# Another order of the first two batches, and q and k transposed in four transfers in place of six

## The chip, the cores and the metric

The kernel runs on one core of one Trainium2 chip. The metric is the device time of one execution in microseconds (us); lower is better. Of four runs of the kernel before, the median is 314.41 us (313.33 to 316.91).

The engines are called as in the profile: PE is TensorE (matmuls), PEld its loading of weights, ACT is ScalarE, DVE is VectorE, POOL is GpSimd, and SP is SyncE, which here only issues transfers. Each engine carries out its own instructions in order.

## The reference

Two layers follow each other. The first is attention over a sliding window, with a bias that falls with the distance; the second multiplies the result x by w_in, applies h * cos(h), and multiplies by w_out.

```python
B, H, S, D = 8, 8, 576, 64                       # q, k, v, float32
scores = scale * q @ k.T + bias                  # bias = -slope[h] * |i - j|
mask = (rel >= 0) & (rel < 128)                  # rel = i - j
attn = softmax(where(mask, scores, -1e9))
x = (attn @ v).transpose(0, 2, 1, 3).reshape(4608, 512)
h = x @ w_in                                     # 512 x 2048
out = (h * cos(h)) @ w_out                       # 2048 x 512
```

## The kernel before, in words

**Tiles.** A batch has 576 tokens: four blocks of 128 and a last one of 64. The 4608 tokens of all batches together are also cut into nine chunks of 512 for the second layer, so chunk c holds the end of one batch and the start of the next, and each chunk shifts by 64 tokens against the batches. Weights and inputs are cast to bf16 while they are loaded.

**Attention.** `load_nat` (line 450) brings q and k with tokens on the partitions, one block at a time, from POOL's queue. They are wanted with the head's 64 columns on the partitions. For batches 0 and 1 TensorE transposes them (`first_transposes`, line 532, and `first_tail`, line 558). For batches 2 to 7 `cross_transposes` (line 580) issues DMA transposes from SP: for each of q and k one transfer for blocks 0 and 1, one for blocks 2 and 3, and one for the short block 4 with its 64 rows. A batch's work is nine units (`units`, line 598): four pairs of heads for the first 256 tokens (G = 0), four for the next 256 (G = 1), and one tail. `scores` (line 608) multiplies for a whole group of units in one piece of PE work (the matmuls are on lines 629 and 619); `exps` (650) is on ACT, `mask` (671) on DVE, `pv` (696) on PE, `norm` (738) on DVE, and `x_back` (775) brings x back with its columns on the partitions: by PE in the first batches, and by a DMA transpose from SP (line 786, the tail line 778) from the second half of batch 2 on. Batches 2 to 7 run in three groups of three units. The second group holds the last pair of heads of G = 0 and the first two of G = 1; for G = 1 the scores need blocks 1 to 3 of k and 2 and 3 of q.

**Second layer.** `moe1` (line 830) multiplies a chunk by 128 columns of w_in in four matmuls of 512 tokens (line 835). `moe1_half` (line 842) does two times 128 columns for 256 of the chunk's tokens instead, in eight matmuls (line 850), so a chunk's first half can start before x of the second half is there. How many column pairs are done in halves is the tuple in the loop at the end (line 925). `gcu` (819) is cos on ACT and the product on DVE; `moe2_mm` (858) is the multiplication by w_out (line 861), and `store` (869) the way out.

**The order of the work.** `Plan` (line 109) sets it before the kernel runs. Each piece of work is written down by `op` with its engine, its reads and writes, a cost in ns (`occ`, `lat`) and a priority (`pri`, small first). `schedule` (198) places the pieces one by one at the earliest time at which an engine can take them, by those costs, and the order found is the fixed order of each engine's instructions. So where a transfer lands later than the plan had it, the engine stands still, and all that was placed behind it waits too. `Wires` (line 51) models the transfers: every packet of a transposing transfer costs 0.92 ns, or 1.45 where POOL's queue runs as well, whose packets cost 0.825 and more; SP is held while over 2000 of its packets are outstanding (RING). `pad` (170) fills PE's waits in the first 16 us with matmuls of zeros.

**Queues.** All loads but two come from POOL in the order of the list `FIRST`, then batch by batch (`load_batch`, line 900): batch 3 behind the last transpose of batch 2, later ones behind the x transposes of an earlier batch. SP issues the transposes of q and k, those of x, and the stores, in the order of the plan.

**The first two batches** follow three lists written out by hand: `HEAD` for batch 0 ("T" a transposition on PE, "R" a group of units with its PSUM slots, "E" the masks of the tail), `JOBS` for the sixteen `moe1_half` of chunk 0 (half, column pair, PSUM bank), and `SECOND` for batch 1 ("F" is the transposition of the short block).

Of the kernel before, what the change touches and what calls it, by code (L numbers as in the profile page):

```python
# [20 lines left out]
SPLIT = 4  # L21
VW = 66

ORDER, WAR, DATA = 0, 1, 2
FIRST = [("k", "q", 0, 1), ("h", "k"), ("h", "q"), ("v", 0, 0), ("v", 0, 1), ("k", "k", 0, 1),
         ("v", 0, 2), ("v", 0, 3), ("i", 6, 2), ("i", 2, 2), ("i", 4, 2), ("i", 0, 2),
         ("i", 12, 2), ("i", 8, 4), ("m",), ("i", 14, 2), ("k", "q", 1, 0), ("v", 0, 4),
         ("t", "k", 0), ("o", 0, 4), ("k", "k", 1, 0), ("t", "q", 0), ("o", 4, 4), ("o", 8, 4),
         ("v", 1, 0), ("v", 1, 1), ("o", 12, 2), ("o", 14, 2), ("v", 1, 2), ("k", "k", 1, 1),
         ("k", "q", 1, 1), ("t", "k", 1), ("t", "q", 1), ("v", 1, 4), ("v", 1, 3)]  # L30
HEAD = [("T", "k", 0, 0, 3), ("T", "q", 0, 2, 3), ("R", (3,), (1,)), ("T", "q", 1, 7, 6),
        ("R", (1,), (2,)), ("R", (0,), (0,)), ("R", (2,), (3,)), ("T", "k", 1, 1, 7),
        ("R", (4,), (0,)), ("E",), ("R", (7,), (3,)), ("R", (5,), (2,)), ("R", (6,), (1,))]
JOBS = [(0, 6, 6), (0, 1, 1), (0, 2, 3), (1, 4, 1), (0, 4, 2), (0, 3, 5), (1, 3, 3), (1, 2, 6),
        (0, 0, 4), (1, 1, 7), (1, 0, 0), (1, 7, 5), (1, 6, 2), (0, 7, 7), (0, 5, 3), (1, 5, 4)]
SECOND = [("T", "k", 0, 2, 2), ("F", 0, 6), ("T", "q", 0, 3, 3), ("R", (2,), (3,)),
          ("R", (9,), (1,)), ("R", (1,), (2,)), ("R", (3,), (3,)), ("T", "k", 1, 6, 6),
          ("T", "q", 1, 4, 4), ("R", (4,), (3,)), ("R", (0,), (1,)), ("R", (7,), (3,)),
          ("F", 1, 5), ("R", (5,), (2,)), ("R", (8,), (1,)), ("R", (6,), (2,))]
ENG = ("pe", "act", "dve", "pool", "sp")  # L40


# [8 lines left out]
class Wires:  # L51
# [4 lines left out]
    CROSS, MIXED = 0.92, 1.45  # L56
    RING = 2000
    LOADED = 3200

    def __init__(self):  # L60
        self.t = 0.0
# [30 lines left out]
    def add(self, o, e, st):  # L92
        if st > self.t:
            self.t, self.q, _ = self._step(self.t, self.q, st)
        n, cost, cross = o.pk
        late = self.LOADED if e != "pool" and self.q.get("pool") else 0
        self.q.setdefault(e, []).append([o, st + o.occ + self.DELAY[e] + late, n, cross, cost])
        _, _, done = self._step(self.t, self._copy(), 1e9)
        free = st + o.occ
        held = sum(x[2] for x in self.q[e])  # L100
        for d, de, t in done:
            d.end = t + (self.DONE if de != "pool" else min(2400, max(0, 0.17 * (t - 3000))))
            if de == e and e != "pool" and held > self.RING:
                held -= next(x[2] for x in self.q[e] if x[0] is d)
                free = max(free, t)
        return free


class Plan:
# [5 lines left out]
    COLD = 7000  # L115
    HEAD = 16000
    SLACK = 25
# [8 lines left out]
    def op(self, eng, fn, r=(), w=(), dma=None, occ=100, lat=None, pri=5, mode=0, table=None,  # L126
           pk=None, after=(), behind=()):
        o = Op()
        o.seq = len(self.all)
        o.eng = (eng,) if isinstance(eng, str) else tuple(eng)  # L130
        o.fn, o.r, o.w, o.dma = fn, tuple(r), tuple(w), dma
        o.occ, o.lat, o.pri, o.mode, o.table = occ, occ if lat is None else lat, pri, mode, table
        o.pk, o.banks = pk, {k[1]: None for k in o.w if k[0] == "B"}
        preds = {d: ORDER for d in behind}
        preds.update((d, DATA) for d in after)
        for k in o.r:
            if k in self.writer:
                preds[self.writer[k]] = DATA
        for k in o.w:
            if k in self.writer:  # L140
                preds[self.writer[k]] = DATA
                if k[0] == "B":
                    o.banks[k[1]] = self.writer[k]
            for d in self.readers.get(k, ()):
                preds.setdefault(d, WAR)
        if dma is not None and dma in self.lastdma:
            preds[self.lastdma[dma]] = DATA
        if eng == "pool":
            if eng in self.lastseq:
                preds.setdefault(self.lastseq[eng], ORDER)  # L150
            self.lastseq[eng] = o
        if dma is not None:
            self.lastdma[dma] = o
        o.preds, o.succs, o.npred = preds, [], len(preds)
        for d in preds:
            d.succs.append(o)
        for k in o.r:
            self.readers.setdefault(k, []).append(o)
        for k in o.w:
            self.writer[k], self.readers[k] = o, []  # L160
        self.all.append(o)
        return o
# [199 lines left out]
def bass_alibi_sliding__then__act_gcu_kernel(  # L362
# [8 lines left out]
    with ExitStack() as ctx:  # L371
# [3 lines left out]
        R = Plan(nc, ctx)  # L375
        op = R.op
# [5 lines left out]
        nat = {w: [sb(f"{w}nat{i}", [128, NBLK, 512]) for i in range(2)] for w in "qk"}  # L382
        tr = {w: [sb(f"{w}t{i}", [128, NBLK, NPAIR, 128]) for i in range(2)] for w in "qk"}
# [120 lines left out]
        def identity():  # L504
            op("dve", lambda e: e.tensor_scalar(ident[:, :], dif[:, 1, :], 0.0, None, ALU.is_equal),
               r=["dif"], w=["ident"], occ=210, lat=280, pri=0)

        def fills():
            for i in range(2):
                op("dve", lambda e, i=i: e.memset(vp[i][:, :, :, 64:65], 1.0), w=[("vinit", i)])  # L510
                op("dve", lambda e, i=i: e.memset(vp[i][64:128, 4, :, 0:64], 0.0),
                   w=[("vinit", i)], occ=280)
                op("dve", lambda e, i=i: e.memset(Pt[i][:, 1024:1088], 0.0), w=[("Pt", i)])
                op("dve", lambda e, i=i: e.memset(tr["k"][i][:, 4, :, 64:128], 0.0),
                   w=[("ktail", i)], occ=170)
            op("dve", lambda e: e.memset(halfpi[:, :], math.pi / 2.0), w=["halfpi"])

        def masks():
# [61 lines left out]
        def cross_transposes(b):  # L580
            i = b % 2
            before = list(xops) if b > 2 else []
            xops.clear()
            crossed.clear()
            for t0, t1 in ((0, 2), (2, 4), (4, 5)):
                for w in "qk":
                    rows = 128 if t0 < 4 else 64
                    o = op("sp", [lambda e, t0=t0, t1=t1, rows=rows, w=w: e.dma_start_transpose(
                        tr[w][i][:, t0:t1, :, 0:rows].rearrange("p t k f -> p (t k) f"),
                        nat[w][i][0:rows, t0:t1, :].rearrange("p t f -> p (t f)"))],  # L590
                       r=[("nat", w, i, t) for t in range(t0, t1)],
                       w=[("tr", w, i, t, hf) for t in range(t0, t1) for hf in range(2)],
                       dma=f"x{w}{i}{t0}", occ=1250, pk=(1024 if t0 < 4 else 256, 0.92, True), pri=3,
                       behind=before)
                    crossed.append(o)

# [282 lines left out]
        def moe2(c):  # L879
            yield  # L880
            for t in range(4):
                cols = [(0, 512, OB[t % 2])] if c < NCH - 1 or t < 3 else [(0, 384, 1), (384, 128, 2)]
                for c0, wd, bank in cols:
# [2 lines left out]

        load_first("q", q, 0, 0, "sp")
        load_first("k", k, 0, 1, "sp")
        distances()
        fills()  # L890
        identity()
        loads = {"k": lambda w, b, g: load_piece(w, {"q": q, "k": k}[w], b, g),
                 "t": lambda w, b: load_nat(w, {"q": q, "k": k}[w], b, 4),
                 "h": lambda w: load_half(w, {"q": q, "k": k}[w], 1),
                 "v": lambda b, t: load_v(b, (t,)),
                 "i": load_w_in, "o": load_w_out, "m": masks}
        for f, *a in FIRST:
            loads[f](*a)

# [22 lines left out]
        for c in range(NCH):  # L922
            turn(1)
            if c:
                n = (0, 8, 6, 6, SPLIT, SPLIT, SPLIT, SPLIT, 0)[c]
                for i in range(2 * n):
                    moe1_half(c, i // n, i % n, 2 + i % 6)
                for i in range(16 - 2 * n):
                    moe1(c, 2 * n + i, 2 + (2 * n + i) % 6)
            second = moe2(c)  # L930
            if c + 1 < B:
                us = units(c + 1)
                if c == 0:
                    play(1, SECOND)
                else:
                    cross_transposes(c + 1)
                    if c == 1:
                        load_batch(3, crossed[-1:])
                    for g in range(0, 9, 3):
                        run(us[g:g + 3], (1, 2, 3))  # L940
            if c == 0:
                load_batch(2)
            elif c + 3 < B:
                load_batch(c + 3, xops[-1:])
            for _ in second:
                pass
# [29 lines left out]
```

The softmax here doesn't subtract the row's maximum and nothing guards it: scores larger than these inputs give would overflow.

## Time and profile before

| what | value |
|---|---|
| median of four runs | 314.41 us (313.33 to 316.91) |
| the profiled execution's own time | 316.91 us |
| its span, first to last instruction | 314.9 us |
| mean granted clock of TensorE | 0.995 |
| read from and written to memory | 36.70 MB and 9.44 MB |
| packets of POOL's queue (q0) | 108992 |
| packets of SP's queue (q1) | 50160 |

A profile page shows one execution. Its first part gives the busy time of each engine; the second cuts the span into 40 slices (of 7.9 us here) and gives for each the busy share in tenths, the clock that TensorE was granted, and the share of the transfer engines. Further views give the waits (who waited for whom), the chain of work that ended last, the instructions in order of time, and sums over stretches of time. A line number names the line of the kernel that issued the work; `x16` is a count. TensorE's busy time is modelled from pipelined matmuls, so it says when it had work and not how well it was used.

### The profile page before, as it was taken

What the parts mean: (1) busy time and instruction counts of PE and PEld (TensorE: products, weight loads), DVE (VectorE), ACT (ScalarE), POOL (GpSimd) and SP (SyncE); (2) the same over time, 40 slices, a digit from 0 to 9 for tenths busy, and PEclk for the clock granted to TensorE, in tenths of its full rate; (3) what the DMA queues carried; (4) which work ended last, traced back from release to release, by engine and by line L of the source; (5) the groups of instructions that cost most, each with busy time, mean ns of one, the idle gap of its engine ahead of it and who ended that gap; (6) DMA issues with size and microseconds to landing.
All of it is one profiled execution on the core that took longest, in us unless ns stands there. A gap on an engine that the chain in (4) does not pass through costs nothing.

```text
span 314.9 us, 6876 instructions
## 1 busy us (share of the span) xinstructions
PE 306.0 (97%) x2748; PEld 184.2 (58%) x2748; DVE 197.4 (63%) x441; ACT 207.0 (66%) x306; POOL 103.6 (33%) x131
## 2 busy tenths in 40 slices
PE   7899999999999997999999999999999999999996
PEld 4487555884577445845764575458545844444444
DVE  4887766785587655867687578758865880363000
ACT  7887846986687664784887488739855883362211
POOL 8999670009608700690059007800000000000000
PEclk9999999999999997999999999999999999999999
DMA  9999999999979997999969999997713100201112
GB/s 133 173 199 188 195 166 197 150 120 139 169 96 141 167 152 120 114 131 173 138 95 154 161 147 130 163 170 128 148 52 100 35 2 11 90 2 67 67 67 102
DMA packets 159183, 38.99 MB, mean 124 GB/s; under 512 B 147760, under 2 KB 154672, under 8 KB 159152
## 3 DMA queue, kind: packets, MB, share of 16 engines
q0 software_dynamic: 108992, 18.10, 78.0%
q1 hardware_dynamic: 50160, 20.46, 34.3%
q8 instruction: 22, 0.36, 0.5%
q14 instruction: 9, 0.07, 0.1%
HBM read 36.70 MB, written 9.44 MB: 146 GB/s over the span
## 4 chain that ended last, share of the span: by engine, by line
PE 85%; DMA 9%; POOL 4%; issue 0%; SPq 0%; ACT 0%; DVE 0%; POOLq 0%
PE ps L861 38%; PE ps L850 21%; PE ps L835 15%; DMA xT<-xnat 5%; PE ps L629 4%; DMA w_inb<-in_moe_w_in_dram 4%; PE ps L723 2%; PE ps L726 1%; POOL w_inb L468 1%; POOL vp L461 1%; PE ps L544 1%; PE ps L709 1%; PE ps L711 1%; PE ps L798 0%; PE ps L619 0%
## 5 line engine op out<-in xcount | busy, mean ns | idle before, releaser
L861 PE MATMUL ps<-w_outb,gT 128*128 128x512 bf16 (+2 forms) x592 | 139.3, 374 | 0.0
L827 DVE TENSOR_TENSOR gT<-ps,cos 128x512 bf16<-128x512 f32 x144 | 95.0, 687 | 32.7 <-PE ps L861 16.3
L821 ACT ACTIVATE cos<-ps,halfpi 128x512 f32<-128x512 f32 x144 | 94.8, 686 | 27.0 <-PE ps L850 11.0
L850 PE MATMUL ps<-xT,w_inb 128*128 128x256 bf16 x704 | 84.6, 274 | 2.8 <-DMA xT<-xnat 2.2
L861 PEld LDWEIGHTS ps<-w_outb,gT 128*128 128x128 bf16 x592 | 52.6, 98 | 52.4 <-issue 1.4
L850 PEld LDWEIGHTS ps<-xT,w_inb 128*128 128x128 bf16 x704 | 66.7, 98 | 13.6 <-DMA xT<-xnat 3.1
L666 ACT ACTIVATE p<-ps 128x768 bf16<-128x768 f32 (+1 forms) x64 | 54.5, 917 | 22.1 <-PE ps L629 12.6
L452 POOL DMA_DIRECT2D qnat<-in_q_dram x32 | 28.8, 899 | 93.5 <-DMA xT<-xtail 68.8
L835 PE MATMUL ps<-xT,w_inb 128*128 128x512 bf16 x224 | 49.7, 379 | 0.0
L417 ACT ACTIVATE ob<-ps 128x512 f32<-128x512 f32 (+2 forms) x24 | 13.9, 581 | 45.6 <-PE ps L861 45.6
L835 PEld LDWEIGHTS ps<-xT,w_inb 128*128 128x128 bf16 x224 | 21.9, 98 | 25.2 <-DVE gT L827 0.5
L461 POOL DMA_DIRECT2D vp<-in_v_dram x40 | 35.0, 941 | 2.2 <-issue 1.2
L684 DVE TENSOR_TENSOR p<-p,emask 128x1024 bf16<-128x1024 bf16 x32 | 21.8, 687 | 14.5 <-ACT p L666 14.2
L452 POOL DMA_DIRECT2D knat<-in_k_dram x32 | 28.9, 904 | 2.9 <-issue 2.9
L765 DVE TENSOR_TENSOR xnat<-ps,rec 128x256 bf16<-128x256 f32 x64 | 26.9, 422 | 2.0
L723 PEld LDWEIGHTS ps<-vp,p 128*128 128x128 bf16 x256 | 17.2, 98 | 13.7 <-issue 8.7
L723 PE MATMUL ps<-vp,p 128*128 128x65 bf16 x256 | 22.1, 194 | 0.1
L726 PE MATMUL ps<-vp,p 128*128 128x65 bf16 x192 | 20.1, 194 | 0.0
L489 ACT ACT_TABLE_LOAD x15 | 19.2, 1283 | 0.3
L689 DVE TENSOR_TENSOR p<-p,emask 128x256 bf16<-128x256 bf16 x32 | 9.0, 282 | 15.6 <-ACT p L666 15.2
L629 PEld LDWEIGHTS ps<-qt,kt 64*128 64x128 bf16 x320 | 11.9, 94 | 11.3 <-issue 7.9
L629 PE MATMUL ps<-qt,kt 64*128 64x128 bf16 (+1 forms) x320 | 17.8, 238 | 0.3 <-ACT kt L417 0.2
(58 smaller groups left out, 170.4 us busy)
## 6 DMA issues: line engine op xcount, KB each, us to landing
out_dram<-ob SPq DMA_DIRECT2D x35, 256.0 KB, 3.6
vp<-in_v_dram POOLq DMA_DIRECT2D x32, 128.0 KB, 12.1
knat<-in_k_dram POOLq DMA_DIRECT2D x25, 128.0 KB, 9.0
qnat<-in_q_dram POOLq DMA_DIRECT2D x25, 128.0 KB, 8.3
w_inb<-in_moe_w_in_dram POOLq DMA_DIRECT2D x6, 256.0 KB, 7.6
w_outb<-in_moe_w_out_dram POOLq DMA_DIRECT2D x3, 512.0 KB, 15.6
qnat<-in_q_dram POOLq DMA_DIRECT2D x3, 256.0 KB, 12.2
knat<-in_k_dram POOLq DMA_DIRECT2D x3, 256.0 KB, 14.1
```

The lines of the kernel that those rows point to most:

```text
L452: op("pool", [lambda e: e.dma_start(nat[w][b % 2][0:rows, t, :].rearrange("p (h d) -> p h d", h=H), src[b, :, 128 * t:128 * t + rows, :].r ...
L461: op("pool", [lambda e, t=t, rows=rows: e.dma_start(vp[b % 2][0:rows, t, :, 0:64], v[b, :, 128 * t:128 * t + rows, :].rearrange("h p d -> ...
L629: ins = e.matmul(ps[:, banks[x], c0:c1], keys_ap(i, x, pr, kc), query_ap(i, x, pr, qb, nb), start=True, stop=True)
L666: op("act", lambda e: e.activation(P[i][:, :, lo:512], src_[:, :, lo:512], ACTF.Exp, scale=0.125), w=held + [("P", i)], occ=920 if u[1] el ...
L723: ins = e.matmul(o, P[i][:, x, d0:d0 + 128], V[:, kc, h, 0:65], start=True, stop=not two)
L726: ins = e.matmul(o, P[i][:, x, p0:p0 + 128], V[:, kc - 1, h, 0:65], start=False, stop=True)
L765: op("dve", lambda e: e.tensor_tensor(o, U[:, :, :, 0:64], rv[:, :, :, None].broadcast_to([128, 2, 2, 64]), ALU.mult), r=[("rec", ri)], w= ...
L821: op("act", lambda e: e.activation(cosb[ci][:, :], h, ACTF.Sin, bias=halfpi[:, 0:1]), r=["halfpi"], w=[("B", bank), ("cos", ci)], occ=586, ...
L827: op("dve", lambda e: e.tensor_tensor(o, h, cs, ALU.mult), r=[("cos", ci)], w=[("B", bank)] + keys, occ=606, lat=692, pri=3)
L835: op("pe", lambda e, kc=kc: e.matmul(ps[:, bank, :], w_in[:, kc, 128 * fc:128 * fc + 128], xT[:, kc, CH * c:CH * c + CH], start=(kc == 0), ...
L850: op("pe", lambda e, i=i, fc=fc, kc=kc: e.matmul(ps[:, bank, 256 * i:256 * i + 256], w_in[:, kc, 128 * fc:128 * fc + 128], xT[:, kc, t0:t0 ...
L861: op("pe", lambda e, fc=fc: e.matmul(ps[:, bank, 0:wd], gT[gi][:, fc, 128 * t:128 * t + 128], w_out[:, fc, c0:c0 + wd], start=(fc == 0), s ...
```

## The change

Four things are changed.

- The transfers of `cross_transposes`: blocks 2, 3 and 4 of q go in one transfer, and so do those of k. The short block 4 is transposed with 128 rows; its lower 64 rows of the source are set to zero once at the start (`fills`), and the zeros that used to be written to the transposed k by a memset (`ktail`) come with the transfer too.
- The lists `FIRST`, `HEAD`, `JOBS` and `SECOND` have a new order. Two loads of weights are cut into smaller pieces, and making the distances and the identity is now an entry of `FIRST` ("d"), still at its head.
- In chunk 3, all eight column pairs are done in halves, in place of six.
- The plan's limit of 2400 ns has a name (`LAG`), with the same value.

```diff
-FIRST = [("k", "q", 0, 1), ("h", "k"), ("h", "q"), ("v", 0, 0), ("v", 0, 1), ("k", "k", 0, 1),
-         ("v", 0, 2), ("v", 0, 3), ("i", 6, 2), ("i", 2, 2), ("i", 4, 2), ("i", 0, 2),
-         ("i", 12, 2), ("i", 8, 4), ("m",), ("i", 14, 2), ("k", "q", 1, 0), ("v", 0, 4),
-         ("t", "k", 0), ("o", 0, 4), ("k", "k", 1, 0), ("t", "q", 0), ("o", 4, 4), ("o", 8, 4),
-         ("v", 1, 0), ("v", 1, 1), ("o", 12, 2), ("o", 14, 2), ("v", 1, 2), ("k", "k", 1, 1),
-         ("k", "q", 1, 1), ("t", "k", 1), ("t", "q", 1), ("v", 1, 4), ("v", 1, 3)]
-HEAD = [("T", "k", 0, 0, 3), ("T", "q", 0, 2, 3), ("R", (3,), (1,)), ("T", "q", 1, 7, 6),
-        ("R", (1,), (2,)), ("R", (0,), (0,)), ("R", (2,), (3,)), ("T", "k", 1, 1, 7),
-        ("R", (4,), (0,)), ("E",), ("R", (7,), (3,)), ("R", (5,), (2,)), ("R", (6,), (1,))]
-JOBS = [(0, 6, 6), (0, 1, 1), (0, 2, 3), (1, 4, 1), (0, 4, 2), (0, 3, 5), (1, 3, 3), (1, 2, 6),
-        (0, 0, 4), (1, 1, 7), (1, 0, 0), (1, 7, 5), (1, 6, 2), (0, 7, 7), (0, 5, 3), (1, 5, 4)]
+FIRST = [("d",), ("k", "q", 0, 1), ("h", "k"), ("h", "q"), ("v", 0, 0), ("m",), ("v", 0, 1),
+         ("k", "k", 0, 1), ("i", 2, 2), ("v", 0, 3), ("v", 0, 2), ("i", 4, 2), ("i", 6, 2),
+         ("i", 12, 2), ("i", 8, 2), ("i", 0, 2), ("k", "q", 1, 0), ("i", 10, 2), ("t", "q", 0),
+         ("i", 14, 2), ("o", 2, 2), ("o", 0, 2), ("k", "k", 1, 0), ("t", "k", 0), ("o", 8, 2),
+         ("o", 4, 4), ("v", 0, 4), ("o", 10, 2), ("v", 1, 0), ("v", 1, 1), ("o", 12, 2),
+         ("o", 14, 2), ("v", 1, 4), ("t", "q", 1), ("k", "k", 1, 1), ("k", "q", 1, 1),
+         ("t", "k", 1), ("v", 1, 3), ("v", 1, 2)]
+HEAD = [("T", "k", 0, 6, 3), ("T", "q", 0, 1, 3), ("R", (3,), (1,)), ("R", (0,), (2,)),
+        ("T", "q", 1, 5, 6), ("R", (1,), (0,)), ("R", (2,), (3,)), ("E",), ("T", "k", 1, 5, 7),
+        ("R", (6,), (0,)), ("R", (4,), (2,)), ("R", (5,), (1,)), ("R", (7,), (3,))]
+JOBS = [(0, 2, 3), (0, 3, 7), (0, 1, 1), (1, 4, 5), (0, 6, 4), (1, 2, 6), (1, 3, 3), (0, 0, 5),
+        (1, 0, 0), (0, 4, 6), (1, 6, 2), (0, 7, 7), (1, 1, 5), (0, 5, 3), (1, 7, 5), (1, 5, 1)]
...
@@ fills
+                for w in "qk":
+                    op("dve", lambda e, i=i, w=w: e.memset(nat[w][i][64:128, 4, :], 0.0),
+                       w=[("blank", w, i)], occ=330, pri=8)
...
@@ cross_transposes
-            for t0, t1 in ((0, 2), (2, 4), (4, 5)):
+            for t0, t1 in ((0, 2), (2, 5)):
                 for w in "qk":
-                    rows = 128 if t0 < 4 else 64
...
-                        tr[w][i][:, t0:t1, :, 0:rows].rearrange("p t k f -> p (t k) f"),
-                        nat[w][i][0:rows, t0:t1, :].rearrange("p t f -> p (t f)"))],
-                       r=[("nat", w, i, t) for t in range(t0, t1)],
-                       w=[("tr", w, i, t, hf) for t in range(t0, t1) for hf in range(2)],
-                       dma=f"x{w}{i}{t0}", occ=1250, pk=(1024 if t0 < 4 else 256, 0.92, True), pri=3,
+                        tr[w][i][:, t0:t1, :, :].rearrange("p t k f -> p (t k) f"),
+                        nat[w][i][:, t0:t1, :].rearrange("p t f -> p (t f)"))],
+                       r=[("nat", w, i, t) for t in range(t0, t1)] + [("blank", w, i)] * (t1 > 4),
+                       w=[("tr", w, i, t, hf) for t in range(t0, t1) for hf in range(2)] +
+                         [("ktail", i)] * (t1 > 4 and w == "k"),
+                       dma=f"x{w}{i}{t0}", occ=1250, pk=(512 * (t1 - t0), 0.92, True), pri=3,
...
-                n = (0, 8, 6, 6, SPLIT, SPLIT, SPLIT, SPLIT, 0)[c]
+                n = (0, 8, 6, 8, SPLIT, SPLIT, SPLIT, SPLIT, 0)[c]
```

`SECOND` is reordered in the same way. Its transpositions, units and PSUM slots are the same kinds of entries.

## The prediction

> **What bounds the kernel now.** I read the page first, then the granted clock, the waits and the chain, and last the transposes one by one. The page's busy row and two of its slice rows:
>
> ```profile
> PE 306.0 (97%) x2748; PEld 184.2 (58%) x2748; DVE 197.4 (63%) x441; ACT 207.0 (66%) x306; POOL 103.6 (33%) x131
> ...
> PEclk9999999999999997999999999999999999999999
> ...
> DMA  9999999999979997999969999997713100201112
> ```
>
> TensorE is busy nearly all the time, and the change leaves its multiplications as they are, so only its waits can move the end. The DMA row stands at 9 up to about 230 us: the transfers have almost no spare room while batches are loaded. The one low digit of the clock belongs to a place that the windows show (columns: stretch, length, busy time and count by engine, then clock, DMA share and GB/s):
>
> ```profile
> 117.80:119.90 2.10, 0.10 (x2) 0.05 (x2) 0.91 (x2) 2.08 (x3) 0.00 (x0) 1.00 1.64 175
> 120.90:124.20 3.30, 3.30 (x29) 2.32 (x27) 2.25 (x6) 0.00 (x0) 0.00 (x0) 0.50 0.19 40
> ```
>
> TensorE is idle for 2.0 us at the start of chunk 3, and then runs 3.3 us at half clock, another 1.65 us lost. The list of waits (us in total, times, longest) names the cause:
>
> ```profile
> PE ps L850 <- DMA xT<-xnat: 2.2, 2, 2.0
> ```
>
> and the chain of work, in order of time, shows the transfer (start, length):
>
> ```profile
> 110.88 8.93 DMA xT<-xnat
> ```
>
> The transfer of one finished x block back into xT needed 8.9 us from issue to landing. The list of waits has also 0.5 us for a late w_in piece (the timeline of TensorE, before 24.38 us). Elsewhere after 20 us I find no wait over 0.5 us.
>
> Now the transposes of q and k. In batch 5 the SP queue and TensorE's second group of scores stand so in the timeline (start, length):
>
> ```profile
> 163.87 2.78 SPq L588 DMA_TRANSPOSE kt<-knat  x1
> 166.69 1.46 SPq L588 DMA_TRANSPOSE qt<-qnat  x1
> 168.21 1.33 SPq L588 DMA_TRANSPOSE kt<-knat  x1
> ...
> 174.60 0.78 PE L629 MATMUL ps<-qt,kt 64*128 64x256 bf16 x16
> ```
>
> The view of line 588, narrowed to the first and the last of these three issues, gives their way to landing:
>
> ```profile
> DMA to landing us min/median/max: 9.2/9.2/9.2
> ...
> DMA to landing us min/median/max: 6.6/6.6/6.6
> ```
>
> So blocks 2 and 3 of k land at 163.87+9.2 = 173.1 and the short block 4 at 168.21+6.6 = 174.8, while the second group starts at 174.60. It needs blocks 1 to 3 and is ready 1.5 us before it starts; it doesn't need block 4, which lands after it has begun.
>
> **The change part by part.**
>
> Removed: two issues on SP for each of batches 2 to 7, some 1.3 us each (their rows above). SP is off TensorE's path and the queue behind it is full, so I count 0. If SP did hold the later x transposes back, two issues would give up to 2.6 us in a batch; that end is kept for a rival.
>
> Added: the last block goes with 128 rows in place of 64, so 64 KB more for q and as much for k, 512 packets of 256 bytes. Bounds of their time: below, batch 7, which nothing loads beside: its transfers of 1024 packets land 1.4 us apart (issues at 223.1 and 224.5, each landing 3.3 us later), so 512 take 0.7 us. Above, the mean of the queue while batch 6 is loaded:
>
> ```profile
> q1 hardware_dynamic: 6457, 2.02, 53.6%
> ```
>
> 6457 packets in the 25 us from 127 to 152, so 512 take 2.0 us. The nearest row is the transposes themselves: landing to landing, 1024 packets take 2.6 to 4.0 us in batches 3 to 6 (mean 3.4), and a short block's 256 take 0.6 to 1.6 (mean 0.96). One merged transfer of 1536 is then 5.1 us where the two took 4.36: 0.74 each, 1.5 us for q and k. I take 1.5.
>
> The Trainium skill, page "DMA: Bandwidth & Descriptors", section "Rules for kernel authors", says to coalesce many small transfers, since under 64 KB one pays mostly overhead; the short blocks are 64 KB. By that rule merging would cost nothing and the sum would be the first rival's; the row speaks against it, since 256 packets took 0.96 us where a quarter of a large transfer takes 0.85.
>
> Moved, and here lies my forecast: blocks 2 and 3 share a semaphore with block 4, so the second group of scores (units 3, 4, 5) waits for the end of the whole. That end is the present landing of k's block 4 plus 1.5 us. Batch by batch, landing of block 4 now / start of the second group now: batch 3 109.4 / 109.55; batch 4 143.7 / 144.34; batch 5 174.8 / 174.60; batch 6 204.6 / 204.84. With 1.5 us the group is late by 1.35, 0.9, 1.7 and 1.25 us: 5.2 together. Batch 2 (71.2 / 78.61) and batch 7 (229.5 / 235.93) are never late. Queued behind the scores on TensorE, which goes in order, are the w_out matmuls that could have filled the time, and then P times V; ACT's exps wait for the scores. With 0.7 us the four are late by 0.55, 0.05, 0.9 and 0.45 (2.0 together), with 2.0 by 1.85, 1.35, 2.2 and 1.75 (7.1). The plan could put w_out matmuls ahead of the group; then the wait costs nothing. It keeps the group 5.5 to 5.6 us behind the first in batches 3 to 7, also where the data are long there, and charges the extra packets at most 1.45+0.825 ns each, 1.2 us; I count nothing covered.
>
> The x transposes of batch 3 stand behind on the same queue: they land some 1.5 us later, and TensorE reaches them 1.35 us later. The wait at 117.6 and the half clock after it stay as they are: 0. In later batches the first half of a chunk needs no x block of the newest batch, which hides 1.5 us; without that cover each such wait would cost up to 1.5.
>
> n of chunk 3 from 6 to 8: 16 matmuls of 512 columns at 216 ns become 32 of 256 at 109 ns: 3.46 against 3.49 us, 0. It puts the work on the second half 2 x 8 x 109 ns = 1.7 us later, but the wait seen is on the first.
>
> Four memsets of 64x512 on VectorE, about 0.27 us each by the row of the equally large V fill: 1.1 us in the first 4 us. If all lay before the first cast (3.66 us), the first transposes were up to 0.8 us later; the upper halves of q and k arrive only at 8.6 us, which covers that. Without that cover: 0.8.
>
> New order of the loads: one more w_in issue and two more w_out issues of POOL, about 0.9 us each. A piece issued between 9 and 13 us lands 6 to 11 us later, so the queue is full and the issues cost 0; if POOL bounded it, 2.7 us. The w_in piece of 512 KB, which TensorE waited for at 24.4 us, is split and stands behind five others that landed every 1.3 us; its 0.7 us (0.53 of idle and the drain) should go, and the first w_in piece comes ahead of two v blocks. The new order of HEAD, JOBS and SECOND shuffles the same work; lost time before 20 us is about 10 us, most of it before the data. I take -1.0 for the start, between +1.5 (a piece of w_out late) and -2.5.
>
> Sum against the profiled execution's own time, 316.91 (a span of 314.9 and 2.0 around it): +5.2 -1.0 = +4.2, 321.1. That execution is the slowest of the four; their median is 2.5 lower, and I move the same +4.2 to it: 314.41 + 4.2 = 318.6.
>
> **The rivals.**
>
> 1. The merged transfers end in time, by less overhead or because the plan fills the wait. For it: the lower bound of 0.7 us leaves only 2.0 us of waits. Against it: the margins above. Only the start's -1.0 is left: 313.4.
>
> 2. Faster: the wait of chunk 3 goes. Place: the x transfer issued at 110.88. With two transfers fewer ahead it would have to land 2.2 us sooner, by 117.6; that is the point from which it decides. Price: 2.2 us and 1.65 of half clock, with rival 1's -1.0: 314.41 - 4.85 = 309.6. For it: two issues less. Against it: 512 more packets in the same queue, and 8.9 us on the way though SP was free.
>
> 3. Slower yet: one of the new waits, 1.7 us at most by my sum, also halves the clock. In the trace 2.0 us idle did so and 0.5 us didn't. Two such stretches of 3.3 us cost 2 x 1.65: 321.9. The Trainium skill, page "TensorE: Matmul & The Clock Gate", section "What's actually happening", lets the clock fall after an idle window of about 3.4 us; by it no wait of this size would be enough, and the sum would stay at 318.6. The trace's 2.0 us was enough, so I keep this rival.
>
> **How the numbers follow.** The main case has 0.44, with a range of its own from 315.4 (waits of 2.0) to 320.5 (waits of 7.1); rival 1 0.30 (311 to 315), rival 2 0.20, rival 3 0.06. About 1% is what a measurement here can tell from no change, 311.3 to 317.6. Faster: rival 2 and 0.03 of rival 1, 0.23. Same: the rest of rival 1 and 0.07 of the main case, 0.34. Slower: 0.37 of the main case and rival 3, 0.43. The range reaches from 310.8, where half of rival 2 is left out, to 320.8, the end of the main case.
>
> **What would show it.** Right: a new row of TensorE waiting for kt or qt transposes, 0.8 to 1.8 us in each of batches 3 to 6, the second group later behind the first than 5.5 us, and the row at 117.6 still there. Wrong: no such row, and the k transfer of blocks 2 to 4 landing no later than block 4 does now; or the half clock gone. The start is right if no wait for w_in is left and chunk 0 ends up to 1 us sooner.

## The result and the profile after

The changed kernel takes 315.98 us (median of 40 runs, 313.14 to 318.86), the kernel before 314.56 (61 runs beside it). The ratio is 1.0036, with a 95% interval of 1.0022 to 1.005: slower by some 0.4%, where I had forecast 1.3% slower, 318.6. The ratio is taken without the slow runs, five of the changed kernel's, all above 318 us; by the two medians it is 1.0045. The direction came out, and the kind of wait; the size is about a third of what I said.

The profiled execution of the changed kernel took 314.96 us, below its median, with a span of 313.1; that of before took 316.91, the second highest of all 61 runs. So the two pages by themselves say the opposite of the medians, and the changed kernel's looks the better one. The waits in its page are those of an execution 1.0 us faster than the median, and can be shorter than what the median execution has:

```profile
PE 303.5 (97%) x2764; PEld 184.7 (59%) x2764; DVE 197.8 (63%) x448; ACT 207.0 (66%) x303; POOL 106.1 (34%) x134
...
PEclk9999999999999999999999999999999999999999
DMA  9999999999999995999899999999913100201112
```

The half clock (the 7 in the row of the clock before) is gone from this execution. TensorE's waits after (us in total, times, longest) show the new wait for k at the top, and a shorter wait for xT:

```profile
PE ps L634 <- DMA kt<-knat: 1.3, 1, 1.3
...
PE ps L855 <- DMA xT<-xnat: 1.1, 1, 1.1
...
PE ps L855 <- DMA w_inb<-in_moe_w_in_dram: 0.2, 1, 0.2
```

The new wait stands in batch 5. The timeline of SP and of TensorE there:

```profile
156.42 1.25 SPq L592 DMA_TRANSPOSE qt<-qnat  x1
158.19 1.23 SPq L592 DMA_TRANSPOSE kt<-knat  x1
159.55 2.45 SPq L592 DMA_TRANSPOSE qt<-qnat  x1
162.10 3.99 SPq L592 DMA_TRANSPOSE kt<-knat  x1
```

```profile
166.16 0.67 PE L634 MATMUL ps<-qt,kt 64*128 64x256 bf16 x12
...
170.32 1.68 PE L866 MATMUL ps<-w_outb,gT 128*128 128x512 bf16 x7
173.27 0.78 PE L634 MATMUL ps<-qt,kt 64*128 64x256 bf16 x16 [1.28 <-DMA kt<-knat]
```

and the view of line 592 for the last of the four issues:

```profile
DMA to landing us min/median/max: 11.1/11.1/11.1
```

162.10 + 11.1 = 173.2: the second group starts the moment the transfer of blocks 2 to 4 lands. In batches 3, 4 and 6 it finds its data there: the merged transfer lands at 98.1+10.5 = 108.6, 129.4+11.4 = 140.8 and 192.3+10.9 = 203.2, and the groups start at

```profile
109.18 0.78 PE L634 MATMUL ps<-qt,kt 64*128 64x256 bf16 x16
...
141.41 0.78 PE L634 MATMUL ps<-qt,kt 64*128 64x256 bf16 x16
...
203.61 0.78 PE L634 MATMUL ps<-qt,kt 64*128 64x256 bf16 x16
```

Batch 5 has two things against it. Its first transfer is issued at 156.42, 9.7 us before the first group of scores starts (166.16, above); in batches 3, 4 and 6 the distance is 10.5, 11.4 and 10.5 us. And its merged transfer lands the latest after the first issue: 16.8 us, against 15.5, 16.2 and 15.7.

### The profile page after: what moved, and what is told of

The parts are those of the page before. It is cut to its first block, busy times and chain, and to the rows that moved or that the text cites. A ratio compares the mean times of both kernels' runs of the same rounds, so it can differ in the third digit from the quotient of the medians.

```text
span 313.1 us, 6892 instructions
## 1 busy us (share of the span) xinstructions
PE 303.5 (97%) x2764; PEld 184.7 (59%) x2764; DVE 197.8 (63%) x448; ACT 207.0 (66%) x303; POOL 106.1 (34%) x134
## 4 chain that ended last, share of the span: by engine, by line
PE 75%; DMA 12%; POOL 8%; SPq 2%; issue 1%; DVE 1%; ACT 0%; POOLq 0%
PE ps L866 34%; PE ps L855 20%; PE ps L840 12%; DMA qnat<-in_q_dram 6%; PE ps L634 4%; DMA kt<-knat 4%; DMA xT<-xnat 2%; POOL vp L463 2%; PE ps L728 2%; POOL w_inb L470 2%; SPq L592 2%; PE ps L731 1%; POOL w_outb L477 1%; POOL knat L427 1%; PE ps L714 1%
## 5 line engine op out<-in xcount | busy, mean ns | idle before, releaser
L855 PE MATMUL ps<-xT,w_inb 128*128 128x256 bf16 x736 | 87.1, 273 | 1.2 <-DMA xT<-xnat 1.1
L855 PEld LDWEIGHTS ps<-xT,w_inb 128*128 128x128 bf16 x736 | 69.3, 98 | 11.6 <-DMA xT<-xnat 1.3
L840 PE MATMUL ps<-xT,w_inb 128*128 128x512 bf16 x208 | 46.0, 379 | 0.0
L840 PEld LDWEIGHTS ps<-xT,w_inb 128*128 128x128 bf16 x208 | 20.3, 98 | 23.6 <-DVE gT L832 0.5
L689 DVE TENSOR_TENSOR p<-p,emask 128x1024 bf16<-128x1024 bf16 x32 | 22.0, 687 | 11.4 <-ACT p L671 11.2
L728 PEld LDWEIGHTS ps<-vp,p 128*128 128x128 bf16 x256 | 17.2, 97 | 13.4 <-issue 9.3
```

The costliest lines, as they stand in the source:

```text
L728: ins = e.matmul(o, P[i][:, x, d0:d0 + 128], V[:, kc, h, 0:65], start=True, stop=not two)
L840: op("pe", lambda e, kc=kc: e.matmul(ps[:, bank, :], w_in[:, kc, 128 * fc:128 * fc + 128], xT[:, kc, CH * c:CH * c + CH], start=(kc == 0), ...
L855: op("pe", lambda e, i=i, fc=fc, kc=kc: e.matmul(ps[:, bank, 256 * i:256 * i + 256], w_in[:, kc, 128 * fc:128 * fc + 128], xT[:, kc, t0:t0 ...
```

## The experiments

T1 is the theory of the prediction: the second group of scores waits for the merged transfer. T2 says that the new order of the first two batches costs the time, T3 that n = 8 in chunk 3 does. The first four kernels make, with before and the changed one, part of a table of all combinations.

**The transfers alone.** The kernel before, with the transfers of the change and the four memsets; the first line of the change stands for the rest.

```diff
-            for t0, t1 in ((0, 2), (2, 4), (4, 5)):
+            for t0, t1 in ((0, 2), (2, 5)):
...
```

> The kernel before with the four merged transfers and their zero rows alone. Theory T1 (the loss sits in the second group of scores of batches 3 to 6, which waits for the merged transfer of k): 1 to 2 us slower than before, with rows of TensorE waiting for kt, the longest 1 to 2 us. Rival T2 (the new order of batches 0 and 1 costs the time): within 0.3 us of before. Rival T3 (n = 8 in chunk 3 costs it): within 0.3 us. If the landing of the last transfer of k, counted from the first issue of the batch, stays at 15.5 to 16.8 us, merging costs the queue little in spite of the added packets.

316.97 us, ratio 1.0077 (1.0045 to 1.0109). T1 holds so far: the transfers alone cost at least as much as the whole change. TensorE's waits for k come to 2.4 us in this execution, and what follows the longest is half clock:

```profile
174.35 0.88 PE L632 MATMUL ps<-qt,kt 64*128 64x256 bf16 x16 [2.13 <-DMA kt<-knat]
```

```profile
174.90:178.30 3.40, 3.40 (x16) 1.26 (x11) 1.32 (x3) 2.64 (x3) 0.00 (x0) 0.50 2.05 167
```

In the second fence, a stretch of the windows, the clock is the third number from the end: 3.4 us at 0.50, 1.7 us lost on top of the wait. Again it is batch 5 that waits; the other 0.2 us are in batch 4.

**The order alone.** The kernel before with the new FIRST, HEAD, JOBS and SECOND; the diff shows the start of HEAD.

```diff
-HEAD = [("T", "k", 0, 0, 3), ("T", "q", 0, 2, 3), ("R", (3,), (1,)), ("T", "q", 1, 7, 6),
+HEAD = [("T", "k", 0, 6, 3), ("T", "q", 0, 1, 3), ("R", (3,), (1,)), ("R", (0,), (2,)),
...
```

> The kernel before with the new lists for batches 0 and 1 alone. T1: as before or up to 1 us faster, since the wait for w_in at 24 us goes. T2: 1 to 2 us slower, with longer waits before 60 us. T3: as T1.

315.13 us, ratio 1.002 (0.9999 to 1.0041). Not the gain of 1.0 us that I had put down for it, and not clearly a loss.

**n alone.** The kernel before with n = 8 in chunk 3.

```diff
-                n = (0, 8, 6, 6, SPLIT, SPLIT, SPLIT, SPLIT, 0)[c]
+                n = (0, 8, 6, 8, SPLIT, SPLIT, SPLIT, SPLIT, 0)[c]
```

> The kernel before with eight in place of six column pairs in halves in chunk 3, alone. T1 and T2: within 0.4 us of before; the wait for xT near 117.6 us stays at 1 to 2.3 us. T3: 1 us or more slower.

314.23 us, ratio 0.9987 (0.9964 to 1.001): T3 falls. Its profile has the old order, and this list of TensorE's waits between 4 and 60 us is all of it:

```profile
PE ps L544 <- ACT kt L417: 0.8, 1, 0.8
PE ps L544 <- DVE qnat L440: 0.3, 1, 0.3
```

No wait for w_in: the one at 24 us that I had read from the profile of before, and counted as a gain of 0.7 us, isn't there in this execution of the same order. It is no accident of one execution either, since e1, in the old order too, has it:

```profile
24.84 7.90 PE L853 MATMUL ps<-xT,w_inb 128*128 128x256 bf16 x69 [0.51 <-DMA w_inb<-in_moe_w_in_dram]
```

Of the six profiles with the old order only these two have a wait for w_in near 24 us.

**Six transfers again.** The changed kernel without the merging and the memsets, the first line again for the rest.

```diff
-            for t0, t1 in ((0, 2), (2, 5)):
+            for t0, t1 in ((0, 2), (2, 4), (4, 5)):
...
```

> The changed kernel with its six transfers back, without the zero rows. T1: the loss is gone, 0 to 1 us faster than before, and TensorE's wait for kt is gone. T2: still 1 to 2 us slower than before. T3: still slower.

314.96 us, ratio 1.0013 (0.999 to 1.0037), with no wait for k. Between the medians the changed kernel loses 1.0 us to the merging; between the ratios it is 0.7, and their intervals overlap, so this pair alone doesn't settle it.

**Six transfers, the last with 128 rows.** The added packets without the merging; the 128 rows and the memsets stay.

```diff
-            for t0, t1 in ((0, 2), (2, 5)):
+            for t0, t1 in ((0, 2), (2, 4), (4, 5)):
```

> The changed kernel with six transfers again, but the short block still sent with 128 rows, so the added packets stay and the merging goes. If packets set the time of the queue (my 1.5 us), the last transfer of k in batches 3 to 6 lands 17 to 18 us after the batch's first issue. If a separate small transfer costs as much as the added packets, it lands at 16.5 us or later here too, against 15.6 with six short ones and 16.1 with four. The second group waits for blocks 2 and 3 alone, so TensorE doesn't wait for kt and the time is that of the kernel with six short transfers, 0 to 1 us faster than the changed kernel; if the added packets hold up the x transposes behind them, it is as slow as the changed kernel.

315.14 us, ratio 1.0024 (1.0008 to 1.0041): like six short ones in the median, and no wait for k in its profile; its ratio lies between theirs and the changed kernel's and can't be told from either. What the packets and the merging do to the queue is in the traces: the landing of a batch's last transfer of k, counted from the first issue of the batch, in one execution each.

| kernel | batch 3 | 4 | 5 | 6 | mean |
|---|---|---|---|---|---|
| before, six short | 15.7 | 16.7 | 15.3 | 15.5 | 15.8 |
| changed, six short | 16.1 | 15.8 | 15.0 | 15.4 | 15.6 |
| changed, six of 128 rows | 18.4 | 16.5 | 16.8 | 16.0 | 16.9 |
| changed, four | 15.5 | 16.2 | 16.8 | 15.7 | 16.1 |
| before, four | 16.1 | 17.0 | 17.2 | 15.5 | 16.5 |

By these five, the packets put the end back by 1.2 us, near my 1.5, and merging gives back 0.4 to 0.8 of it. But most of that is batch 3 of a single execution: without it the six of 128 rows have a mean of 16.4, the two kernels with four 16.2 and 16.6. And six short ones can be as late there: e2 has 18.0 in batch 3. So whether a transfer of its own costs the queue anything is not shown. All profiles of this document with six short transfers in every batch, and all with four, six kernels of each kind and one execution of each kernel, say more (mean, and range):

| transfers | batch 3 | 4 | 5 | 6 | mean |
|---|---|---|---|---|---|
| six short | 16.7 (15.7 to 18.0) | 16.0 (15.5 to 16.7) | 15.6 (15.0 to 16.3) | 15.5 (15.4 to 15.6) | 15.9 |
| four | 15.9 (15.3 to 16.5) | 16.5 (16.0 to 17.0) | 17.0 (16.6 to 17.2) | 15.5 (14.9 to 16.1) | 16.2 |

The change in the transfers moves the end by -0.7, +0.5, +1.4 and 0.0 us: in batch 5 nearly the whole of my 1.5, and there in every execution; elsewhere little or nothing. Why the batches differ so was not followed up.

**n = 6 again.** The changed kernel with `(0, 8, 6, 6, ...)`.

```diff
-                n = (0, 8, 6, 8, SPLIT, SPLIT, SPLIT, SPLIT, 0)[c]
+                n = (0, 8, 6, 6, SPLIT, SPLIT, SPLIT, SPLIT, 0)[c]
```

> The changed kernel with n = 6 in chunk 3. Theory that n = 8 takes up part of what the merged transfers cost: 0.5 to 1.2 us slower than the changed kernel, 316.5 to 317.2, with a longer wait for xT near 117 us. Rival: n does nothing, within 0.4 us of the changed kernel's 316.0.

316.58 us, ratio 1.0062 (1.0039 to 1.0085), 0.6 above the changed kernel, at the low edge of what the first theory gave, and within the noise of the two ratios. In this execution batch 5 waits for k for 2.0 us, and the clock stays full:

```profile
172.00:175.20 3.20, 1.19 (x8) 0.34 (x8) 0.57 (x3) 0.60 (x1) 0.29 (x1) 1.00 1.59 190
175.20:178.70 3.50, 3.34 (x34) 1.89 (x36) 1.54 (x5) 2.64 (x3) 0.00 (x0) 1.00 2.04 163
```

**Six transfers in batch 5 alone.** Its short block goes with 64 rows there.

```diff
-            for t0, t1 in ((0, 2), (2, 5)):
+            for t0, t1 in (((0, 2), (2, 4), (4, 5)) if b == 5 else ((0, 2), (2, 5))):
...
```

> The changed kernel with six short transfers in batch 5 alone and four in the others. If batch 5, which has the least time between the first issue and its second group, carries nearly all of the merging's cost: as fast as the changed kernel with six transfers everywhere, 314.7 to 315.3, and no wait for kt over 0.5 us. Rival: the cost is spread over batches 3 to 6: 315.5 to 316.0.

314.9 us, ratio 1.0027 (1.0011 to 1.0043). The median is that of six transfers everywhere, as the theory of batch 5 had it; the ratio, with its interval, can't tell it from the changed kernel's 1.0036. What the profile adds: the waits of the weight loads for k are 0.9 us in two places, none over 0.5, and no matmul waits for k.

**The old order with four transfers and n = 8.** The lists of before, the rest as changed.

```diff
+HEAD = [("T", "k", 0, 0, 3), ("T", "q", 0, 2, 3), ("R", (3,), (1,)), ("T", "q", 1, 7, 6),
-HEAD = [("T", "k", 0, 6, 3), ("T", "q", 0, 1, 3), ("R", (3,), (1,)), ("R", (0,), (2,)),
...
```

> The kernel before with the merged transfers and n = 8, in the old order. If n = 8 takes up part of the merging's cost: 315.5 to 316.3, against 317.0 with n = 6. Rival, that the new order does it: 316.8 to 317.2.

316.72 us, ratio 1.0066 (1.0042 to 1.009): n does little here, so the rival stands. Its profile has two waits for k, 0.7 us in batch 3 and 0.9 in batch 5, so batch 5 is not always the only one that waits. That closes the table of ratios:

| | n = 6 | n = 8 |
|---|---|---|
| six, old order | 1 | 0.9987 |
| six, new order | 1.002 | 1.0013 |
| four, old order | 1.0077 | 1.0066 |
| four, new order | 1.0062 | 1.0036 |

Merging costs 0.2 to 0.8% in every pair, n = 8 gains 0.1 to 0.3%, and the order costs 0.2 to 0.3% beside six transfers and gains 0.15 to 0.3% beside four. Single entries are good to about 0.2 to 0.3%, so three of the four costs of merging are clear of the noise (the pair with the new order and n = 8 is not), while those of n and of the order are not, one by one.

**The wait without the merging.** The changed kernel with six short transfers, as above, and the scores of a batch's second half made to wait for block 4, which they don't use.

```diff
...
                      for t in range(max(0, 2 * G - (w == "k")), 2 * G + 2)]
+            if b >= 2 and G:
+                keys += [("tr", w, i, 4, hf) for w in "qk"]
```

> The changed kernel with six short transfers, in which the scores of the second half of a batch also wait for block 4 of q and k, which they don't use. If the shared semaphore is what merging costs: slower than six transfers (1.0013) and near the changed kernel (1.0036), 315.3 to 316.2, with a wait of TensorE for kt or qt in batch 5 of 0.3 to 1.5 us. If it is the added packets: as six transfers, 314.6 to 315.1, and no such wait.

314.93 us, ratio 1.0017 (0.9979 to 1.0054), and no wait for k in the profile. My theory as stated would have had one. The interval is too wide to say that the wait for block 4 costs nothing: it holds the ratios of six transfers and of the changed kernel, and four of the twelve executions took over 317 us at a mean clock of 0.995, for a reason that no profile shows; the profiled one took 313.68. For that one the timeline of batch 5 shows why it lost nothing:

```profile
172.81 2.32 PE L865 MATMUL ps<-w_outb,gT 128*128 128x512 bf16 x10
175.07 0.78 PE L631 MATMUL ps<-qt,kt 64*128 64x256 bf16 x16
```

The plan took a separate block 4 to be late, and put more matmuls of w_out ahead of the group: it starts 6.7 us behind the first, in place of 5.5, and TensorE works through. So what costs would be a wait that the plan did not see. For the merged transfer its constants give a landing 15.8 us after the first issue (8.4 until the transfer of q starts, 2 x 1536 packets at 2.275 ns, 0.35 for the end); in batch 5 the traces with four transfers have 16.6 to 17.2.

**The same transfers, planned later.** The changed kernel, with 1.2 us added in the plan to the landing of the merged transfers. What changes is the order of the engines' work; one instruction also moves from ACT to VectorE (the pages count 303 and 448 there in the changed kernel, 302 and 449 here).

```diff
             d.end = t + (self.DONE if de != "pool" else min(self.LAG, max(0, 0.17 * (t - 3000))))
+            if d.dma[:2] in ("xq", "xk") and d.dma[-1] == "2":
+                d.end += 1200
```

> The changed kernel, all its instructions kept; only the plan takes the second transfers of q and k to land 1.2 us later than before, and so places w_out matmuls ahead of the second group. If what costs the time is a wait that the fixed order didn't foresee: the wait for kt in batch 5 is gone or under 0.5 us and the time falls to that of six transfers, 314.6 to 315.3. Rival, that the later data or the added packets cost the time by themselves: still 315.7 to 316.3.

313.81 us, ratio 0.9966 (0.9939 to 0.9994): 2.2 us below the changed kernel in the median, and faster than before. TensorE's wait for k is gone; these are the first of TensorE's waits, and the list has none for kt or xT:

```profile
PE ps L551 <- DMA knat<-in_k_dram: 1.7, 2, 1.3
PE ps L416 <- DVE zero L415: 1.2, 1, 1.2
PE ps L551 <- ACT kt L421: 0.6, 1, 0.6
```

The four transfers landed about as late as in the changed kernel (16.1, 16.0, 16.6 and 15.3 us after the first issue). With the data as late as before and the loss gone, the time was lost to an order that came too early for them. The kernel gains more than the 1.0 us that I gave. The wait for xT of chunk 3 isn't in this profile either; it is 1.1 us in the changed kernel's and in that of six transfers, which this kernel beats by 1.15 us in the median. That fits, but how much of the gain belongs to which wait I haven't separated.

**Two tries for a better kernel.** Before with n = 8 in chunks 2 and 3:

```diff
-                n = (0, 8, 6, 6, SPLIT, SPLIT, SPLIT, SPLIT, 0)[c]
+                n = (0, 8, 8, 8, SPLIT, SPLIT, SPLIT, SPLIT, 0)[c]
```

> The kernel before with eight column pairs in halves in chunks 2 and 3, no other change; a version that might beat both. If the late x transposes of batches 2 and 3 are covered by more work that needs only the first half: 0.3 to 1 us faster than before, 313.6 to 314.3. If the waits lie in the first half itself: within 0.3 us.

313.84 us, ratio 0.9968 (0.9943 to 0.9994): faster than before and than the changed kernel. And the same with the merged transfers, planned 1.2 us later as above:

> The old order of batches 0 and 1, the four merged transfers with the later landing in the plan, and eight column pairs in halves in chunks 2 and 3. If merging brings SP and the queue anything, once its wait is foreseen: faster than the same with six transfers (0.9968), 312.5 to 313.5. If merging brings nothing by itself: 313.5 to 314.5.

314.93 us, ratio 0.9997 (0.997 to 1.0024). Here merging brings nothing; TensorE still waits for k twice, 1.1 us together, in batches 5 and 6. 1.2 us of lateness was not enough in this order.

## Why the prediction was right or wrong, point by point

**The new wait: right in kind and in batch 5, absent in the others.** I had four waits of 1.35, 0.9, 1.7 and 1.25 us, 5.2 together. The changed kernel's profile has one, 1.3 in batch 5, where I had the largest; the other kernels with four transfers and the old plan have 2.4 (e1), 2.0 (e6) and 1.6 us (e7) in all, nearly all of it in batch 5 but for e7. Two steps of the sum failed. The first is that the end of every batch is "the present landing of k's block 4 plus 1.5 us": over six kernels of either kind that end moved by -0.7, +0.5, +1.4 and 0.0 us in batches 3 to 6. The 1.5 itself is about right where it was paid; what was wrong was to put it on every batch. The page "DMA: Bandwidth & Descriptors" of the Trainium skill, section "Rules for kernel authors", by which I had nothing left of the cost, fits batches 3 and 6 and not batch 5; and its rule speaks of transfers under 64 KB, where the short blocks have 64. The second step is "I count nothing covered": the data of batch 4 came 0.5 us later, and the margin of 0.6 us covered it. In batch 6 the plan also moved the second group by 0.2 us (5.65 us behind the first, 5.46 before).

**The start, -1.0: wrong.** The order alone gives +0.2%, not clear of zero, and not a gain. The w_in wait at 24 us stands in two of six profiles of the old order, 0.5 us each, so I had counted an occasional stall as a sure one; and the new order has waits of its own, for w_in among them (0.2 us in the changed kernel and in e2). The "about 10 us" of lost time before 20 us are not in the windows either: they show 3.6 us without work, and with the multiplications of zeros it is 8. The memsets, with or without the new order, delay the first transposition from 4.41 to 4.77 us, less than I had allowed; e5, which has them, is 0.2 us slower in the median than e4, which doesn't, and that is within the noise.

**Chunk 3, "0" for n and for the wait at 117.6: not quite.** n = 8 gains 0.1 to 0.3% where I had none, in all four pairs but in none of them beyond the noise. The wait of 2.0 us with half clock behind it was a rare case of the kernel before: the execution that showed it was among its slowest, and of the 110 executions of before that ran beside the experiments nine had a mean clock under 0.999, whatever the place. The wait after is 1.1 us. Rival 2, which was to gain by losing it, did not come about; the median of before can hardly have contained the half clock.

**Rival 1** was nearly right in three batches of four, **rival 3** in one profile: in e1 a wait of 2.1 us was followed by half clock.

**The sum** was +4.2 us. Measured: merging +1.0 us between medians in the new order with n = 8, and +2.4 in the old with n = 6; the order a loss of 0.2 to 0.3% with six transfers and a gain of 0.15 to 0.3% with four, so about 0; n about -0.4 us. Why merging costs more in the old order is not settled; half clock in e1's profile is a part of it.

## What to carry to other kernels

When an order fixed beforehand meets a transfer that lands a little late, the price here was the lateness beyond what the plan foresaw, and for the most part only where the margin was smallest; so look for the batch with the least time, and for whether the plan knows. A change of the transfers calls for new landing times in the plan: nearly the same instructions, in an order planned for a landing 1.2 us later, turned 0.4% slower into 0.3% faster. A stall in a single profile says neither how often it comes nor how long it is in the median execution, so a gain should not be read from it until several executions have been looked at.

## What the runs showed of the hardware

The length of a wait of TensorE does not by itself say whether the clock falls after it. 2.0 us in before and 2.1 in e1 were followed by 3.3 and 3.4 us at half clock, while 2.0 us in the changed kernel with n = 6 were not, nor 1.3 us in the changed kernel. In e11 a wait of 1.3 us was followed by half clock, which set in about 2 us after it:

```profile
13.31 0.41 PE L551 MATMUL ps<-ident,knat 128*64 128x128 bf16 x8 [1.34 <-DMA knat<-in_k_dram]
```

```profile
11.90:15.20 3.30, 1.96 (x40) 1.36 (x38) 2.18 (x8) 2.07 (x6) 3.30 (x5) 1.00 1.89 170
15.30:18.60 3.30, 3.23 (x34) 2.03 (x34) 2.92 (x9) 3.30 (x4) 3.30 (x6) 0.50 1.46 192
```

The Trainium skill, page "TensorE: Matmul & The Clock Gate", section "What's actually happening", has the activity counted in free-running windows of about 3.4 us; that fits a stretch of 3.3 to 3.4 us and a result that depends on where the wait falls, though not a need for a fully idle window: TensorE was busy for 2.0 of the 3.3 us ahead of e11's half clock.

In SP's queue, beside the loads, two transfers of 1536 packets of 256 bytes in place of two of 1024 and two of 256 moved the end of a batch by -0.7 to +1.4 us, batch by batch, with 0.3 in the mean of four batches and six kernels of each kind.
